# Sliding-window attention and an MLP in one kernel: taking the first batch's early casts off GpSimd, with new planning constants

## The chip, the cores and the metric

The kernel runs on one core of a Trainium2 chip. The metric is the device time of one execution in microseconds (us), as a median of several executions. The engines are called by their names in the profile: PE (TensorE matmul), PEld (its weight loads), DVE (VectorE), ACT (ScalarE), POOL (GpSimd) and SP (SyncE, which here only issues DMAs).

## The reference

Attention over 8 batches, 8 heads, 576 tokens and head dimension 64, with a causal window, and behind it a two-layer MLP on the joined heads:

```python
scores = scale * np.matmul(q, k.transpose(0, 1, 3, 2))
mask_plain = (rel >= 0) & (rel < 32)                          # heads 0..3
mask_dil = (rel >= 0) & (rel < 32 * 4) & (rel % 4 == 0)       # heads 4..7
scores = np.where(masks[None, :, :, :], scores, -1000000000.0)
attn = softmax(scores)                # written out with max, exp and sum
x = (attn @ v).transpose(0, 2, 1, 3).reshape(4608, 512)
h = x @ w_in                          # 512 -> 2048
out = np.maximum(0.01 * h, h) @ w_out # 2048 -> 512, float32
```

Inputs and output are float32; the kernel casts to float16 for the matmuls.

## The kernel before

**A planner writes the order of the work.** No loop order is given by hand. Each piece of work (a cast, a transpose, a group of matmuls, a DMA) is added as a task with an engine or several engines to choose from, a duration, a latency and the tasks it depends on. `forward` simulates the engines and appends tasks to each engine's list; `backward` works out how late each could begin; after `PASSES` rounds the shortest simulated schedule is kept, and its order is the program that each engine executes, first in, first out. A task with several engines goes to the one that is free, unless another would end it over 0.02 us earlier. From the time `CALM` on (38.8 us in the plan), durations are multiplied by `MARGIN` of the engine and latencies by `MARGIN['LAND']`. `WHEN` gives first priorities to the eight batches. So a changed duration or margin can move any task on any engine, with no line of its own in the diff.

**The loads come in a fixed order** on SP, with two of them on ACT's queue: `FIRST = 'r0 q01 v01 . q00 w0 v00 . w1 ...'`. Here `r0` is the last 64 tokens (512 to 575) of all heads of batch 0, tile `rest`; `q01` is q and k of group 1 of batch 0, the dilated heads; `q00` those of group 0, the plain heads; `v..` the same for v; `w0` to `w15` are the sixteen pieces of `w_in` and `w_out`, of which `w15` is the last.

**From a load to the scores.** float32 data land in staging tiles `stg` (q, k), `vst` (v) or, for the weights, in tiles not yet used otherwise (`gt`, `xt`, `wst`). A cast (L373 on DVE and POOL, L371 on ACT) writes float16 into `nat`, `rest`, `slots` or `w_in`/`w_out`. For batches 0 and 1, PE transposes `nat` (L640, into the banks `tp` and `fps`) and `rest` (L683), and copies (L386 on DVE, L384 on ACT) bring the result into `slots`, from which the scores are computed (L757 adds the mask, L761 multiplies). Exp on ACT (L768), sums and values on PE (L779), a reciprocal by Ln and Exp on ACT (L804, L806) and a product on DVE (L817, into `xt`) end a unit. There are two units for each pair of heads, and the pairs are taken in the order 2, 3 (dilated), 0, 1 (plain).

**The MLP.** `U` tasks (L836, L865) multiply `xt` by `w_in`, ACT applies the leaky ReLU into `gt` (L851, L877), and `D` tasks multiply `gt` by `w_out`: the first four token tiles plainly (L902, in four parts each, the last of which needs `w14` and `w15`), the others with a seven-product scheme (L992, sums L978 on DVE). The last three chunks do the first matmul by seven products as well (L1261); for that, four sums of the weights are formed on DVE (L1187).

**Which casts the change touches.** In `load_qk`, batch 0's casts (`first`) may go to POOL, DVE or ACT: 8 casts of 128x512, of which four belong to group 1. In `load_rest`, the four casts of 64x256 take the default of `cast`, POOL or DVE, for both early batches. The casts of v and of the weights are separate calls.

Of the kernel before, what the change touches and what calls it, by code (L numbers as in the profile page):

```python
# [16 lines left out]
WIN = 32  # L17
ROOM, LATE = 256, 0.5
RAMP = 0.0
WHEN = (0.0, 0.0, 40.0, 70.0, 100.0, 125.0, 150.0, 180.0)  # L20
PASSES = 9
MARGIN = {'ACT': 1.02, 'DVE': 1.062, 'POOL': 1.0, 'PE': 1.0, 'SP': 1.0, 'DMA': 1.133, 'LAND': 1.15}
CALM = 38.8
SEEDS = ()


def _margin(name, at):
    return MARGIN[name] if at > CALM else 1.0
FIRST = ('r0 q01 v01 . q00 w0 v00 . w1 w2 w3 w4 w5 w6 w7 w8 w9 w10 q11 w11 r1 v11 . w12 '
# [40 lines left out]
class _Plan:  # L70
# [5 lines left out]
    def add(self, eng, dur, lat, deps, fn, prio, soft=0.0, kind=""):  # L76
        choices = eng if isinstance(eng, tuple) else ((eng, dur),)
        t = _Task(choices, lat, deps, fn, prio, soft, len(self.tasks), kind)
        self.tasks.append(t)
        return t  # L80
# [169 lines left out]
def kernel(  # L250
# [14 lines left out]
    B, H, S, D = q.shape  # L265
# [20 lines left out]
    def at(tl, p0, p1, off, *dims):  # L286

        row = tl.ap[0][0]
        return bass.AP(tensor=tl.tensor, offset=tl.offset + p0 * row + off,
                       ap=[[row, p1 - p0]] + [list(d) for d in dims])  # L290

    def dram(t, off, *dims):
        return bass.AP(tensor=t.tensor, offset=t.offset + off, ap=[list(d) for d in dims])
# [61 lines left out]
    def load(queue, dst, src, n, size, deps, prio, late=None, slow=1.0):  # L355
        eng = ENG[queue]
        t = plan.dma(queue, 0.65, took(n, size) * slow, deps,
                     lambda e: eng.dma_start(dst, src), prio,
                     ((0.5 if prio < -1400 else LATE) if late is None else late)
                     + (RAMP * max(0.0, prio + 1500) / 40 if prio < -1400 else 0.0))  # L360
        t.fixed = prio < -1400
        t.rows = n / 16 + 2
        return t

    def cast(dst, src, n, deps, prio, engines=("POOL", "DVE"), slow=1.0):
        cost = {"POOL": 0.15 + n * 0.00102 * slow, "DVE": 0.07 + n * (0.00055 if slow == 1.0 else 0.0011),
                "ACT": (0.06 + n * 0.00087) * slow}

        def fn(e):
            if e == "ACT":  # L370
                nc.scalar.copy(out=dst, in_=src)  # L371
            else:
                ENG[e].tensor_copy(out=dst, in_=src)  # L373
        return add(tuple((e, cost[e]) for e in engines), None, 0.2, deps, fn, prio, 0.0, "cast")
# [18 lines left out]
    def ring(name, n, users):  # L393

        r = rings.setdefault(name, [])
        waits = r[-n] if len(r) >= n else []
        r.append(users)
        return (len(r) - 1) % n, waits
# [30 lines left out]
    def load_qk(b, g, prio):  # L429

        early, first = b < EARLY, b == 0
        base = (b * H + 4 * g) * HS
        stage, loads = [], []
        for o, src in ((0, q), (1, k)):
            if early:
                sn, s_old = ring("STG", NST, s_users := [])
            else:
                if "STG4" not in rings:
                    assert len(rings["STG"]) == 2 * NST
                    rings["STG4"] = rings["STG"][-NST:-1]  # L440
                sn, s_old = ring("STG4", NST - 1, s_users := [])
            st = stg[sn]
            if first and g == 1:
                lo = [load("ACT" if o else "SP", at(st, 0, 128, j * 256, [512, 2], [1, 256]),
                           dram(src, base + j * HS, [4 * D, 128], [2 * HS, 2], [1, 256]),
                           256, 1024, s_old, prio + 0.3 * j + 0.1 * o) for j in range(2)]
            elif early:
                lo = [load("SP", at(st, 0, 128, 0, [256, 4], [1, 256]),
                           dram(src, base, [4 * D, 128], [HS, 4], [1, 256]),
                           512, 1024, s_old, prio + 0.1 * o)] * 2  # L450
            else:
                lo = [load("SP", at(st, 32 * a, 32 * a + 32, 0, [32, 36], [1, 32]),
                           dram(src, base + (a // 2) * 2 * HS + (a % 2) * 32,
                                [D, 32], [32 * D, 36], [1, 32]),
                           1152, 128, s_old, prio) for a in range(4)]
            stage.append((st, s_users))
            loads.append(lo)
        for j in range(2):
            nn, n_old = ring("NAT", NNAT, n_users := [])
            na, c_qk = nat[nn], []  # L460
            for o in range(2):
                st, s_users = stage[o]
                if early:
                    dst = at(na, 0, 128, o * 512, [D, 2], [128, 4], [1, D])
                    src = at(st, 0, 128, j * 256, [512, 2], [D, 4], [1, D])
                    c = cast(dst, src, 512, [loads[o][j]] + n_old, prio,
                             ("POOL", "DVE", "ACT") if first else ("POOL", "DVE"))
                else:
                    c = cast(na[:, o * S:o * S + S], st[:, j * S:j * S + S], S,
                             loads[o] + n_old, prio, ("POOL",))  # L470
                c_qk.append(c)
                s_users.append(c)
            raw[b, 2 * g + j] = na, c_qk, n_users

    def load_rest(b, prio, queue="SP"):
        _, r_old = ring("REST", 1, r_users := [])
        sn, s_old = ring("STG", NST, s_users := [])
        st, c = stg[sn], []
        for o, src in ((0, q), (1, k)):
            lo = load(queue, at(st, 0, 64, o * 512, [64, 8], [1, 64]),  # L480
                      dram(src, b * H * HS + 512 * D, [D, 64], [HS, 8], [1, D]),
                      512, 256, s_old, prio + 0.1 * o)
            c += [cast(at(rest, 0, 64, o * 512 + 256 * g, [128, 2], [64, 2], [1, D]),
                       at(st, 0, 64, o * 512 + 256 * g, [64, 2], [128, 2], [1, D]), 256, [lo] + r_old, prio)
                  for g in (1, 0)]
        s_users += c
        raw[b, "rest"] = c, r_users
# [636 lines left out]
    for i, step in enumerate(steps):  # L1124
        kind, prio = step[0], clock[0] + 1 + i
# [11 lines left out]
    def attend(b, first, step):  # L1137
        if b >= EARLY:
            take_slots(b)
            for n, g in enumerate((1, 0)):  # L1140
                load_qk(b, g, first + 2 * step * n - 12)
                load_v(b, g, first + 2 * step * n - 11)
        for n, vi in enumerate(VISITS):
            if b < EARLY and n == b:
                turn_rest(b, first + step * n)
            turn(b, vi, first + step * n)
        if b == 0:
            banks = {2: three + [fps[0]], 3: three + [fps[0]], 0: three + hps[1:], 1: three + hps[1:]}
        else:
            banks = dict.fromkeys(VISITS, three + hps if b == 1 else three)  # L1150
        for n, vi in enumerate(VISITS):
            for u in range(2):
                unit(b, vi, u, first + step * n + 0.5 * step * u, banks[vi])
# [4 lines left out]
    def ups(c, x, n, batches):  # L1158
        if n == 192:
            pool = hps  # L1160
            for j in range(0, NJ, 2):
                up_pair(c, j, x, n, batches, all_acts[c], pool[j // 2 % len(pool)])
            return
        for j in range(NJ):
            wide_j = c == 0 and j in wide_banks
            ht = wide_banks[j] if wide_j else hps[h_at[0] % 2]
            h_at[0] += not wide_j
            up(c, j, x, n, batches, all_acts[c], ht, c == 0)
# [182 lines left out]
    for m in range(B // 2):  # L1351
        for c in range(3 * m, 3 * m + 3):
            gt_free[c] = []
        e, o = 2 * m, 2 * m + 1
        attend(e, WHEN[e], (WHEN[e + 1] - WHEN[e]) / 4 if e else 1.0)
        if 3 * m not in U_SEVEN:
# [3 lines left out]
        if m == 0:  # L1360
# [3 lines left out]
            ups(1, 0, 192, [e])  # L1364
            attend(o, WHEN[o], 5.0)
            ups(1, 192, 192, [o])
        else:
            attend(o, WHEN[o], 6.5)
            if 3 * m + 1 not in U_SEVEN:
# [23 lines left out]
    for t, u in zip(pe, pe[1:]):  # L1393
# [3 lines left out]
        while t.start > 0.5 and x + 0.3 < u.start:  # L1397
            n, step = (512, 0.3) if x + 0.4 < u.start else (256, 0.2)
# [41 lines left out]
```

## Time and profile before

| | us |
|---|---|
| median of 3 executions | 299.82 (299.55 to 300.49) |
| the profiled execution, its own time | 299.23 |
| span of its first to last instruction | 297.3 |
| busy in the span: PE / DVE / ACT / POOL | 285.0 / 221.7 / 218.9 / 142.7 |
| mean granted TensorE clock | 0.994 |

A timeline row gives the start, the time taken, the engine, the line, the operation, what it writes and reads, the shape and the count; several instructions of a kind in a row are merged. Brackets hold the idle time of the engine before it and what ended that. A `q` behind an engine's name is its sequencer, so `SPq DMA_DIRECT2D` is the issue of a transfer.

### The profile page before, as it was taken

To read this page: it belongs to the slowest core of one execution; us is meant where nothing else is said; L and a number is where in the kernel's file an instruction comes from. 1 tells how busy PE (TensorE), PEld (TensorE's weight loads), DVE (VectorE), ACT (ScalarE), POOL (GpSimd) and SP (SyncE) were. 2 spreads that over 40 slices of the span, in tenths; PEclk is the share of its full clock that TensorE was granted. 3 is DMA by queue.
4 is the path that set the end of the run, shared out by engine and by line. 5 is a ranking of instruction groups with operands and counts; after the bars stand their busy time and mean duration, and the time that the engine had idled before them with its cause. 6 is when DMAs were issued, how large, how long until landed. Compare 5 with 4: busy or idle time off the path is not lost.

```text
span 297.3 us, 7789 instructions
## 1 busy us (share of the span) xinstructions
PE 285.0 (96%) x2975; PEld 226.4 (76%) x2975; DVE 221.7 (75%) x406; ACT 218.9 (74%) x502; POOL 142.7 (48%) x201
## 2 busy tenths in 40 slices
PE   5779999999999999999999999998999999999995
PEld 2655677578667788777777787776789999999984
DVE  6785385986799899839768879899657786587742
ACT  1797578678988875878878866886877787877611
POOL 5455454197787848937866749996000100000000
PEclk9799999999999999999999999999999999999999
DMA  7999999889889988979899999440101210111033
GB/s 216 330 320 403 344 362 217 147 163 190 169 167 200 208 183 178 207 155 197 178 199 172 203 192 161 137 126 2 36 19 54 75 36 2 37 71 39 35 108 106
DMA packets 155973, 47.16 MB, mean 159 GB/s; under 512 B 136736, under 2 KB 153248, under 8 KB 155936
## 3 DMA queue, kind: packets, MB, share of 16 engines
q1 hardware_dynamic: 155248, 46.04, 65.1%
q10 hardware_dynamic: 688, 0.63, 0.7%
q8 instruction: 23, 0.38, 0.5%
q14 instruction: 14, 0.11, 0.1%
HBM read 37.22 MB, written 9.44 MB: 157 GB/s over the span
## 4 chain that ended last, share of the span: by engine, by line
PE 79%; DMA 8%; DVE 6%; ACT 3%; issue 2%; POOL 1%; SPq 0%; DVEq 0%; POOLq 0%
PE hps L836 22%; PE fps L992 22%; PE tp L992 8%; PE hps L1261 5%; PE ops L1261 3%; DMA xt<-in_moe_w_out_dram 3%; PE ops L779 3%; DMA vst<-in_v_dram 3%; PE fps L902 3%; PE ops L761 2%; PE hps L865 2%; DMA stg<-in_k_dram 2%; PE sps L779 2%; ACT gt L851 1%; DVE slots L386 1%
## 5 line engine op out<-in xcount | busy, mean ns | idle before, releaser
L836 PE MATMUL hps<-xt,w_in 128*128 128x384 f16 x488 | 95.1, 326 | 0.8 <-ACT gt L851 0.8
L992 PEld LDWEIGHTS <-gt 128*128 128x128 f16 x768 | 72.5, 98 | 9.5
L851 ACT ACTIVATE gt<-hps 128x384 f16<-128x384 f32 x122 | 59.1, 491 | 20.0 <-PE hps L836 18.8
L836 PEld LDWEIGHTS <-w_in 128*128 128x128 f16 x512 | 45.9, 98 | 23.2 <-issue 1.2
L373 POOL CAST slots<-vst 64x576 f16<-64x576 f32 (+2 forms) x60 | 54.4, 920 | 7.6 <-DVE slots L386 2.9
L992 PE MATMUL fps<-w_out,gt 128*128 128x256 f16 x368 | 47.0, 273 | 0.0
L373 POOL CAST nat<-stg 128x576 f16<-128x576 f32 (+1 forms) x55 | 40.6, 761 | 12.1 <-DVE xt L817 6.1
L772 DVE TENSOR_TENSOR ee<-ee,con 128x384 f16<-128x384 f16 (+1 forms) x48 | 23.7, 495 | 15.0 <-ACT ee L768 14.8
L806 ACT ACTIVATE rc<-rc 128x288 f32<-128x288 f32 x64 | 27.9, 442 | 0.9
L817 DVE TENSOR_TENSOR xt<-ops,rc 128x288 f16<-128x288 f32 x40 | 18.0, 450 | 12.7 <-ACT rc L806 8.3
L386 POOL COPY slots<-turned 64x64 f16<-64x64 f16 (+2 forms) x36 | 18.6, 525 | 15.1 <-DVE turned L605 7.5
L761 PEld LDWEIGHTS <-slots 128*128 128x128 f16 x320 | 18.7, 99 | 6.5 <-issue 1.4
L788 POOL TENSOR_TENSOR ee<-ee 128x128 f16<-128x128 f16 x9 | 5.3, 586 | 33.9 <-DVE ee L772 29.0
L779 PEld LDWEIGHTS <-slots 128*128 128x128 f16 x320 | 17.8, 97 | 4.7 <-POOL w_in L373 1.0
L768 ACT ACTIVATE ee<-ops 128x384 f16<-128x384 f32 (+1 forms) x39 | 19.5, 504 | 2.2 <-PE ops L761 1.8
L1021 ACT COPY stg<-fps 128x512 f32<-128x512 f32 (+1 forms) x24 | 12.8, 531 | 11.1 <-PE fps L992 10.4
L804 ACT ACTIVATE rc<-ops 128x288 f32<-128x288 f32 x39 | 15.8, 408 | 6.0 <-PE ops L796 3.1
L384 ACT COPY slots<-turned 64x512 f16<-64x512 f16 (+1 forms) x28 | 18.6, 663 | 1.9 <-DVE turned L605 1.5
L1288 ACT ACTIVATE gt<-slots 128x384 f16<-128x384 f32 x36 | 18.3, 526 | 0.9 <-DVE slots L1281 0.7
L605 DVE STREAM_TRANSPOSE turned<-nat 128x576 f16<-128x576 f16 x24 | 17.9, 760 | 0.0
L978 DVE TENSOR_TENSOR gt<-gt 128x1024 f16<-128x1024 f16 x21 | 17.2, 821 | 0.2 <-PE fps L992 0.2
L1261 PEld LDWEIGHTS <-stg 128*128 128x128 f16 x192 | 16.3, 98 | 0.3
(137 smaller groups left out, 556.6 us busy)
## 6 DMA issues: line engine op xcount, KB each, us to landing
out_dram<-osb SPq DMA_DIRECT2D x32, 256.0 KB, 2.5
stg<-in_q_dram SPq DMA_DIRECT2D x48, 144.0 KB, 3.4
stg<-in_k_dram SPq DMA_DIRECT2D x48, 144.0 KB, 3.2
vst<-in_v_dram SPq DMA_DIRECT2D x14, 288.0 KB, 4.3
gt<-in_moe_w_in_dram SPq DMA_DIRECT2D x6, 512.0 KB, 6.7
vst<-in_v_dram SPq DMA_DIRECT2D x24, 128.0 KB, 2.9
stg<-in_q_dram SPq DMA_DIRECT2D x3, 512.0 KB, 9.0
stg<-in_k_dram SPq DMA_DIRECT2D x3, 512.0 KB, 9.4
```

Source lines behind the costliest of these rows:

```text
L373: ENG[e].tensor_copy(out=dst, in_=src)
L384: nc.scalar.copy(out=dst, in_=src)
L386: ENG[e].tensor_copy(out=dst, in_=src)
L761: nc.tensor.matmul(p_bank[:, c:c + w], slot(tn, KB + 128 * s, 0, 128, [1, 128]), slot(tn, qx, 0, 128, *qd), start=first or not by_pe, stop ...
L768: lambda e: nc.scalar.activation(out=et[:, 0:n], in_=p_bank[:, 0:n], func=AF.Exp, scale=SCALE), prio)
L772: lambda e: nc.vector.tensor_tensor(out=et[:, 0:n], in0=et[:, 0:n], in1=con[:, table:table + n], op=ALU.mult), prio,
L779: nc.tensor.matmul(at(dst, 0, 128, o, *od), lhs(s), et[:, c:c + w], start=i == 0, stop=i == len(steps) - 1, skip_group_check=True)
L806: lambda e: nc.scalar.activation(out=rt, in_=rt, func=AF.Exp, scale=-1.0), prio)
L836: nc.tensor.matmul(ht[:, 0:n], at(w_in, 0, 128, vi * DFF + j // 2 * 256 + j % 2, [2, 128]), at(xt[m % 2], 0, 128, vi * 1152 + x0 + x, [1, n]),
L851: lambda e: nc.scalar.activation(out=gt[c % NG][:, j * n_c + x:j * n_c + x + n], in_=ht[:, 0:n], func=AF.Prelu, alpha=0.01),
L992: nc.tensor.matmul(bk[:, x:x + HN], tl[:, off + j * step:off + j * step + 128], rhs(j), start=first and x == 0 and j == 0, stop=j == HJ - ...
L1261: nc.tensor.matmul(b[:, i * HT:i * HT + HT], lhs(v, j0 + i), rhs(v), start=first and i == 0 and v == 0, stop=i == 1 and v == 1, skip_group ...
```

## The change

Batch 0's casts of the dilated heads' q and k, and of the last tokens, no longer have POOL among their engines: they may go to DVE or ACT. Batch 1's casts keep theirs. In the planner, a DVE cast of q, k, last tokens or weights counts 0.07 + n * 0.00076 us in place of 0.07 + n * 0.00055, so 0.46 in place of 0.35 us at n = 512. Beside it, constants of the planner differ: from `CALM` on, durations on DVE count 1.099 times (1.062 before), on POOL 1.001 times, latencies 1.129 times (1.15 before); `CALM` itself is 35.4 us (38.8 before), and the first priority of batch 5 is 126.4 (125.0 before).

```diff
-WHEN = (0.0, 0.0, 40.0, 70.0, 100.0, 125.0, 150.0, 180.0)
+WHEN = (0.0, 0.0, 40.0, 70.0, 100.0, 126.4, 150.0, 180.0)
 PASSES = 9
-MARGIN = {'ACT': 1.02, 'DVE': 1.062, 'POOL': 1.0, 'PE': 1.0, 'SP': 1.0, 'DMA': 1.133, 'LAND': 1.15}
-CALM = 38.8
+MARGIN = {'ACT': 1.02, 'DVE': 1.099, 'POOL': 1.001, 'PE': 1.0, 'SP': 1.0, 'DMA': 1.133, 'LAND': 1.129}
+CALM = 35.4
...
     def cast(dst, src, n, deps, prio, engines=("POOL", "DVE"), slow=1.0):
-        cost = {"POOL": 0.15 + n * 0.00102 * slow, "DVE": 0.07 + n * (0.00055 if slow == 1.0 else 0.0011),
+        cost = {"POOL": 0.15 + n * 0.00102 * slow, "DVE": 0.07 + n * (0.00076 if slow == 1.0 else 0.0011),
                 "ACT": (0.06 + n * 0.00087) * slow}
...
                     c = cast(dst, src, 512, [loads[o][j]] + n_old, prio,
-                             ("POOL", "DVE", "ACT") if first else ("POOL", "DVE"))
+                             (("DVE", "ACT") if g else ("POOL", "DVE", "ACT")) if first else ("POOL", "DVE"))
...
             c += [cast(at(rest, 0, 64, o * 512 + 256 * g, [128, 2], [64, 2], [1, D]),
-                       at(st, 0, 64, o * 512 + 256 * g, [64, 2], [128, 2], [1, D]), 256, [lo] + r_old, prio)
+                       at(st, 0, 64, o * 512 + 256 * g, [64, 2], [128, 2], [1, D]), 256, [lo] + r_old, prio,
+                       ("POOL", "DVE") if b else ("DVE", "ACT"))
                   for g in (1, 0)]
```

## The prediction

> **What bounds the kernel now.** I read the page first, then the busy time by stretches, then who PE waits for, then the timeline of the first 15 us, and last the chain of waits with the timelines around the places where it leaves PE.
>
> ```profile
> PE 285.0 (96%) x2975; PEld 226.4 (76%) x2975; DVE 221.7 (75%) x406; ACT 218.9 (74%) x502; POOL 142.7 (48%) x201
> 0.00:10.00 10.00, 5.47 (x26) 2.10 (x27) 6.96 (x14) 2.35 (x5) 5.92 (x15) 1.00 0.81 249
> 10.00:20.00 10.00, 8.87 (x127) 7.40 (x127) 7.86 (x18) 9.03 (x23) 5.40 (x10) 0.83 1.00 307
> 20.00:30.00 10.00, 8.31 (x88) 5.56 (x87) 6.05 (x14) 8.28 (x21) 4.79 (x7) 1.00 1.02 398
> 30.00:50.00 20.00, 19.98 (x222) 14.80 (x222) 11.65 (x28) 14.53 (x36) 9.97 (x15) 1.00 1.10 324
> 70.00:90.00 20.00, 19.27 (x195) 13.57 (x194) 16.34 (x30) 18.06 (x45) 15.28 (x22) 1.00 0.94 178
> 200.00:210.00 10.00, 9.04 (x82) 6.38 (x80) 10.00 (x19) 6.71 (x16) 5.94 (x7) 1.00 0.08 28
> 210.00:230.00 20.00, 20.00 (x238) 17.25 (x237) 13.14 (x31) 15.25 (x38) 0.43 (x1) 1.00 0.06 20
> ```
>
> The columns behind the length are busy us of PE, PEld, DVE, ACT and POOL, then the granted clock, the DMA engines' busy share and GB/s. PE is the bound from 30 us on: it lacks 0.02 us of 20 between 30 and 50, 0.73 between 70 and 90, 0.96 between 200 and 210. Before 30 us it lacks 4.53 + 1.13 + 1.69 = 7.35 us. The matmuls are fixed work, so the end moves only by PE's lost time: nearly all that can be had lies in the first 30 us, where the change works, and what it may spoil lies behind them.
>
> The start shows who holds PE up:
>
> ```profile
> 5.27 0.49 DVE L373 CAST rest<-stg 64x256 f16<-64x256 f32 x2 [0.77 <-DMA stg<-in_q_dram]
> 6.45 0.28 DVE L373 CAST rest<-stg 64x256 f16<-64x256 f32 x1 [0.70 <-DMA stg<-in_k_dram]
> 6.48 0.84 POOL L373 CAST rest<-stg 64x256 f16<-64x256 f32 x1 [2.45 <-DMA stg<-in_k_dram]
> 6.66 2.06 DVE L373 CAST nat<-stg 128x512 f16<-128x512 f32 x2
> 7.28 1.16 POOL L373 CAST nat<-stg 128x512 f16<-128x512 f32 x2
> 7.46 0.29 PE L683 MATMUL hps<-con,rest 64*128 64x64 f16 x4
> 7.78 0.27 ACT L384 COPY slots<-hps 128x128 f16<-128x128 f16 x1 [5.76 <-PE hps L683]
> 8.78 0.40 PE L640 MATMUL tp<-con,nat 128*128 128x128 f16 x4 [1.03 <-DVE nat L373]
> 9.46 0.58 ACT L384 COPY slots<-fps 64x512 f16<-64x512 f16 x1 [0.19 <-DVE slots L386]
> 10.31 0.47 PE L757 MATMUL sps<-con 128*128 128x192 f16 x3
> L373 DVE CAST nat<-stg x2: 411/1068/1726, 6.7 to 7.0; 128x512 f16<-128x512 f32 x2
> L373 POOL CAST nat<-stg x2: 605/605/605, 7.3 to 7.8; 128x512 f16<-128x512 f32 x2
> ```
>
> The last two rows group the casts of that stretch by line (least, median and most ns, first and last start). The two DVE casts are alike, yet one took 0.411 us and the other, from 7.0 to 8.72, 1.726 us: just while POOL cast `rest` (to 7.32) and two halves of `nat` (to 8.44). PE's transposes wait for it at 8.78, DVE's copies queue behind it, and the first scores come at 10.31.
>
> **The change part by part.**
>
> *First casts.* Eight go: four of 64x256, four of 128x512, of which POOL had one and two. On DVE a small one takes 0.28 (row 6.45), a large one 0.411 unopposed. On ACT a large one has this row:
>
> ```profile
> L371 ACT CAST nat<-stg x1: 610/610/610, 15.5 to 15.5; 128x512 f16<-128x512 f32 x1
> ```
>
> For ACT's 64x256 in this layout there is no row; I bound it by 0.27 (its 128x128 copy at 7.78) and 0.58 (its 64x512 copy at 9.46) and take 0.35, near the smaller, since the elements per row are 256 against 128 and 512. If both engines take one of k's last tokens at 6.45, these end near 6.8 in place of 7.32, and the transposes at 7.46 can begin at about 6.9. DVE then casts from 6.75: the four large ones end at about 7.15, 7.55, 7.95 and 8.35 if ACT takes none. The data are there: the casts of before had begun by 7.0 and, for POOL's second, by 7.28 + 0.605 = 7.9. The half of q for which PE waits at 8.78 is third of the four at worst, done at 7.95 rather than 8.72, and second at best, done at 7.55. So PE's transposes of it come 0.8 to 1.2 us earlier. ACT's added casts are covered by its idle time of 5.76 us before 7.78; a large one taken at 7.2 would hold ACT's first copies until 7.8, where they begin now, so it costs nothing even then. If DVE still has its fourth cast to do when the copies are ready, they wait another 0.41. First scores: 1.0 us earlier, between 0.4 and 1.2.
>
> Here a rule of the Trainium skill can be weighed. The row says that a DVE cast lost 1.726 - 0.411 = 1.3 us to three POOL casts in turn. SBUF — State Buffer, section "SBUF: two separate sides", says that VectorE in a two-port mode and GpSimd hold a shared port pair exclusively for a whole instruction, whoever starts first. By that rule alone the DVE cast would be held only by the cast in progress, to 7.32, and would have ended at about 7.75, so the change would bring 0.2 us; by the row it brings about 1.0, and the row decides.
>
> *From there to 30 us.* The chain of dependent work (copies, exp, reciprocals, DVE's products) starts earlier as a whole. It stays ahead of the weights:
>
> ```profile
> 27.16 0.87 POOL L373 CAST w_in<-wst 128x512 f16<-128x512 f32 x1 [0.61 <-DMA wst<-in_moe_w_in_dram]
> 29.99 2.85 PE L836 MATMUL hps<-xt,w_in 128*128 128x384 f16 x16 [0.82 <-ACT gt L851]
> ```
>
> The last cast of `w_in` is done at 28.03; PE's use of it, from 29.99, waits for ACT's evictions instead, so 1.0 us earlier it still finds its weights, with 0.96 to spare. The casts of v on POOL stay, and no large DVE cast of the first group stands beside them now. Full gain at 30 us: 1.0.
>
> *30 to 51 us, where some is given back.*
>
> ```profile
> 41.02 9.40 DMA xt<-in_moe_w_out_dram
> 50.47 0.88 POOL w_out L373
> 51.39 0.38 PE fps L902
> 50.51 1.26 PE L902 MATMUL fps<-w_out,gt 128*128 128x512 f16 x4
> 52.00 1.02 PE L902 MATMUL fps<-w_out,gt 128*128 128x512 f16 x4
> 52.86 0.34 PE L757 MATMUL ops<-con 128*128 128x64 f16 x3
> 53.22 0.34 PE L757 MATMUL hps<-con 128*128 128x384 f16 x2
> ```
>
> The first three rows are of the chain of waits (start, us, what), the others of PE's timeline. The loads keep the DMA engines full (share 1.10), so the last weight piece lands at 50.42 whatever the casts do. PE issues three matmuls of a group from 50.51 and the fourth, which needs that piece, at 51.39; the group takes 1.26 us where the next takes 1.02: a stall of 0.24. A PE that comes early can use that, and whatever of batch 1's scores (the work at 52.86 and 53.22) moves ahead of it: from 52.86 to 53.22 is 0.36 for each, and batch 1 has three such units open, 1.1 us at most, as far as ACT and DVE, which are also earlier, have copied its q and k. So 0.24 to 1.0 of the gain passes. I take 0.75, nearer the upper end, since PE lacks 0.02 of 20 us here now and so has a queue of work rather than gaps: given back 0.25.
>
> *The costs and margins.* These move the order behind 35 us. What they can win or lose there has these rows:
>
> ```profile
> PE ops L761 <- DVE xt L817: 0.7, 1, 0.7
> PE ops L779 <- ACT rc L804: 0.6, 1, 0.6
> PE sps L761 <- DVE xt L817: 0.2, 1, 0.2
> 194.38 1.61 DVE stg L1187
> 197.87 1.66 DVE stg L1187
> ```
>
> These are PE's waits behind 60 us (total, times, longest), then two pieces of the chain. DVE is 10.00 of 10 us busy between 200 and 210, and PE waits there for its products twice, 0.7 + 0.2 = 0.9. Counting DVE 3.5% longer sets PE's users of DVE results later in the list, with other matmuls before them, which is the right direction for those 0.9; but the new order is another order, and one more weight sum of 1.66 us ahead of a product that PE needs would cost as much. Bounds -0.9 and +1.66; I take -0.25, since PE has other work in the list to put there (from 210 to 230 us it is busy without a gap). `WHEN` and POOL's 1.001 I cost at nothing: they change a priority that later rounds replace, and POOL's durations by 0.1%.
>
> *Sum:* -1.0 + 0.25 - 0.25 = -1.0. The profiled execution's own time is 299.23, of which 297.3 is span and 1.9 lies around it, unchanged; it would come to 298.2. It lies 0.59 below the median of the runs shown, 299.82; by that median, the forecast is 298.8.
>
> **The rivals.**
>
> *The DMA hides it.* All but the 0.24 us stall is lost in front of the last weight piece at 51.39, and the margins do nothing. For it: the share of 1.10 and the chain, which passes through that transfer. Against it: PE has no gap before that point, so the work between is not exhausted. Time 299.82 - 0.24 = 299.6, or up to 299.0 if half passes. Chance 0.26.
>
> *DVE becomes the late bound.* The planner, with longer DVE times, puts one of the four weight sums (1.66 us) ahead of a product for which PE waits between 194 and 207 us. It decides once PE's wait for `xt` there exceeds 0.9 + 1.0 us, the gain. With little of the front gain kept that is 299.82 + 1.66 - 0.24 = 301.2; with two sums and the front's 0.75, 302.4; with one and 0.75, 300.7. For it: DVE is already full there, 10.00 of 10. Against it: only 0.9 of PE's time is lost to that now, and the sums have 10 us of room before. Chance 0.21.
>
> *The late waits vanish as well.* If the 0.9 us behind DVE and the 0.6 behind ACT go, this adds 1.25 to the forecast: 297.6. Chance 0.12.
>
> *The clock rises earlier.* Between 10 and 20 us the granted clock is 0.83 in the mean, and like groups of matmuls are slower at first:
>
> ```profile
> 10.62 0.48 PE L761 MATMUL sps<-slots 128*128 128x96 f16 x5
> 14.41 0.33 PE L761 MATMUL ops<-slots 128*128 128x96 f16 x5
> ```
>
> A mean of 0.83 over 10 us is half rate for 3.4 of them, so a full rate would save PE at most 1.7 us; its work there alternates with ACT's exps, which would not be faster, so I let 0.7 pass: 298.1. Against it: the idle 1.03 us before 8.78 only shrinks. The Trainium skill (TensorE: Matmul & The Clock Gate, "What's actually happening") says that activity in a free-running window of about 3.4 us sets the rate, so that its place may differ from run to run; the 3.4 us above agree with its length. Chance 0.05.
>
> **How the numbers follow.** The forecast (298.2 to 298.9) has 0.36. A measurement of this kernel tells about 0.3%, 0.9 us, from no change. Faster by more: forecast, late waits and clock, 0.36 + 0.12 + 0.05 = 0.53. Within: the DMA case, 0.26. Slower: 0.21. The range from 297.4 to 301.3 takes in the late waits (297.6) and the DVE case with one sum (301.2), and leaves out two sums and both extra gains together.
>
> **What would show it.** In the profile after: no POOL cast before v's at about 9.4; no DVE cast over 0.5 us before 9; the first L640 on `tp` by 8.0 and the first scores (L757) near 9.3 rather than 10.31; PE's U work on the second half of `w_in` from about 29.0; the last weight piece landing still near 50.4, with PE's wait before it under 0.5. Wrong would be: first scores after 10.0 (ACT or DVE took too long), a wait of over 0.7 us before 51.4 (the DMA hides it), or PE waits for `xt` of over 1.9 us between 194 and 210.

## The result: slower by 3.7 us, and the profile after

| | before | changed |
|---|---|---|
| median of 6 executions each | 299.69 (299.02 to 301.25) | 303.43 (302.69 to 304.08) |
| changed / before | | 1.0118, 95% interval 1.0089 to 1.0147 |
| the profiled execution, its own time | 299.23 | 304.08 |
| its span | 297.3 | 302.3 |
| busy PE / DVE / ACT / POOL | 285.0 / 221.7 / 218.9 / 142.7 | 284.5 / 227.7 / 217.6 / 141.9 |

The forecast was 298.8, with a range from 297.4 to 301.3. The sign is wrong, and the time lies outside the range.

The busy time by stretches of the changed kernel, in the columns explained with the forecast (length, then PE, PEld, DVE, ACT, POOL, granted clock, DMA share, GB/s):

```profile
0.00:10.00 10.00, 5.79 (x39) 2.71 (x40) 5.60 (x14) 3.57 (x7) 4.02 (x13) 1.00 0.80 244
10.00:20.00 10.00, 6.94 (x109) 5.24 (x107) 7.77 (x18) 8.95 (x23) 4.63 (x8) 1.00 1.08 342
20.00:30.00 10.00, 9.04 (x93) 5.97 (x93) 6.30 (x15) 8.52 (x22) 5.83 (x8) 1.00 1.03 403
30.00:50.00 20.00, 19.46 (x217) 14.53 (x217) 10.25 (x24) 14.49 (x35) 12.18 (x20) 1.00 1.10 315
50.00:70.00 20.00, 18.90 (x215) 13.70 (x213) 16.11 (x25) 13.63 (x32) 10.22 (x16) 1.00 0.80 137
70.00:90.00 20.00, 18.95 (x197) 13.79 (x195) 15.13 (x29) 16.33 (x42) 14.55 (x20) 1.00 0.92 173
130.00:150.00 20.00, 19.24 (x179) 14.05 (x178) 15.65 (x22) 14.97 (x35) 14.10 (x21) 1.00 0.93 197
150.00:170.00 20.00, 19.07 (x198) 14.20 (x198) 15.05 (x29) 16.47 (x37) 11.18 (x17) 1.00 0.94 173
170.00:190.00 20.00, 18.58 (x189) 14.47 (x188) 18.20 (x28) 13.07 (x32) 13.09 (x18) 1.00 0.80 145
200.00:210.00 10.00, 9.92 (x96) 7.23 (x95) 10.00 (x14) 9.45 (x21) 8.19 (x9) 1.00 0.37 94
```

And three stretches of the kernel before, which the forecast did not show:

```profile
130.00:150.00 20.00, 20.00 (x197) 14.88 (x196) 15.95 (x28) 16.00 (x38) 14.55 (x22) 1.00 0.90 178
150.00:170.00 20.00, 20.00 (x209) 15.16 (x206) 15.06 (x29) 16.70 (x40) 13.59 (x20) 1.00 0.97 195
170.00:190.00 20.00, 20.00 (x205) 15.85 (x203) 17.17 (x30) 14.59 (x34) 14.55 (x17) 1.00 0.91 179
```

Read the PE column as lost time. Behind 30 us the kernel before loses 1.78 us of PE in all its stretches. The changed one loses 6.45: 0.54 + 1.10 + 1.05 up to 90 us, 0.76 + 0.93 + 1.42 between 130 and 190 where before lost nothing, 0.08 between 200 and 210, and 0.24 and 0.33 in two stretches not shown (110 to 130, 210 to 230). That is 4.67 of the 5.0 us by which the two spans differ. (The medians differ by 3.7: the profile of before is of a quick execution, that of the changed kernel of the longest of its six.) The other 0.3 is there at 30 us already: the second half of `w_in` is used from 30.30, where it was 29.99. So the place to look is behind 30 us. There the change moves no named cast. It has only numbers of the planner, and so another order.

The timeline of the changed kernel has the new waits of PE; each row's bracket is PE's idle time before it and what ended that (lines stand one higher than before: L817 is now L818, L978 is L979):

```profile
51.95 0.34 PE L758 MATMUL ops<-con 128*128 128x64 f16 x3 [1.10 <-DVE xt L818]
88.23 1.05 PE L993 MATMUL tp<-w_out,gt 128*128 128x256 f16 x8 [0.59 <-DVE gt L979]
150.93 0.35 PE L762 MATMUL sps<-slots 128*128 128x64 f16 x5 [1.68 <-DVE xt L818]
184.51 1.05 PE L993 MATMUL fps<-wst,gt 128*128 128x256 f16 x8 [1.29 <-DVE gt L979]
...
146.03 3.17 DVE L386 COPY slots<-turned 64x64 f16<-64x64 f16 x1
149.22 0.69 DVE L979 TENSOR_TENSOR gt<-gt 128x1024 f16<-128x1024 f16 x1
149.82 0.68 DVE L1030 TENSOR_TENSOR osb<-fps,stg 128x512 f32<-128x512 f32 x1
150.42 0.45 DVE L818 TENSOR_TENSOR xt<-sps,rc 128x288 f16<-128x288 f32 x1
...
146.02 0.69 POOL L612 COPY slots<-turned 128x576 f16<-128x576 f16 x1
146.67 2.50 POOL L373 CAST nat<-stg 128x576 f16<-128x576 f32 x4
...
181.57 2.89 DVE L979 TENSOR_TENSOR gt<-rest,gt 128x1024 f16<-128x1024 f16 x1
181.27 0.83 POOL L373 CAST slots<-vst 64x576 f16<-64x576 f32 x1
182.03 2.96 POOL L373 CAST nat<-stg 128x576 f16<-128x576 f32 x4
```

The two longest, 1.68 and 1.29 us, have one cause in sight. At 146.03 a DVE copy of 64x64, which takes 0.16 us at its shortest, takes 3.17; it ends just after a run of five POOL operations, at 149.17. At 181.57 a sum of a kind that takes 0.68 at 180.36 takes 2.89: it was ready in the midst of a POOL cast of v and waited through it and through three of the four casts behind. In the first case the product `xt` for which PE waits stands three places behind the copy in DVE's queue. It is the signature that the forecast saw at 7.0 us before, now at a place where PE has nothing else to do. The view counts the held time as busy DVE, and DVE shows 6.0 us more busy than before with two instructions fewer.

### The profile page after: what moved, and what is told of

The parts are those of the page before. It is cut to its first block, busy times and chain, and to the rows that moved or that the text cites. A ratio compares the mean times of both kernels' runs of the same rounds, so it can differ in the third digit from the quotient of the medians.

```text
span 302.3 us, 7787 instructions
## 1 busy us (share of the span) xinstructions
PE 284.5 (94%) x2974; PEld 225.3 (75%) x2974; DVE 227.7 (75%) x404; ACT 217.6 (72%) x499; POOL 141.9 (47%) x206
## 4 chain that ended last, share of the span: by engine, by line
PE 63%; DVE 10%; SPq 6%; issue 6%; ACT 5%; DMA 5%; POOL 4%; POOLq 0%; ACTq 0%
PE fps L993 16%; PE hps L837 14%; SPq L358 6%; PE tp L993 6%; PE hps L1262 5%; PE fps L903 4%; PE hps L866 4%; PE ops L1262 3%; DMA stg<-in_k_dram 3%; DVE gt L979 2%; POOL nat L373 2%; PE ops L780 2%; ACT gt L852 2%; DVE slots L386 1%; POOL slots L373 1%
## 5 line engine op out<-in xcount | busy, mean ns | idle before, releaser
L373 POOL CAST slots<-vst 64x576 f16<-64x576 f32 (+2 forms) x62 | 52.4, 856 | 12.6 <-DVE nat L373 5.4
L373 POOL CAST nat<-stg 128x576 f16<-128x576 f32 (+1 forms) x53 | 38.9, 758 | 16.8 <-DVE t L933 7.9
L773 DVE TENSOR_TENSOR ee<-ee,con 128x384 f16<-128x384 f16 (+1 forms) x48 | 25.2, 525 | 8.8 <-ACT ee L769 8.3
L818 DVE TENSOR_TENSOR xt<-ops,rc 128x288 f16<-128x288 f32 x40 | 17.7, 444 | 15.5 <-ACT rc L807 14.3
L789 POOL TENSOR_TENSOR ee<-ee 128x128 f16<-128x128 f16 x13 | 8.2, 629 | 35.5 <-DVE ee L773 35.4
L1022 ACT COPY stg<-fps 128x512 f32<-128x512 f32 (+1 forms) x22 | 11.6, 528 | 13.6 <-PE fps L993 10.6
L993 PE MATMUL fps<-wst,gt 128*128 128x256 f16 x128 | 16.4, 272 | 1.3 <-DVE gt L979 1.3
L979 DVE TENSOR_TENSOR gt<-gt 128x1024 f16<-128x1024 f16 x21 | 16.7, 797 | 0.9 <-PE fps L993 0.9
```

The costliest lines, as they stand in the source:

```text
L773: lambda e: nc.vector.tensor_tensor(out=et[:, 0:n], in0=et[:, 0:n], in1=con[:, table:table + n], op=ALU.mult), prio,
L979: lambda e: ENG[e].tensor_tensor(out=dst, in0=a, in1=b, op=op),
L993: nc.tensor.matmul(bk[:, x:x + HN], tl[:, off + j * step:off + j * step + 128], rhs(j), start=first and x == 0 and j == 0, stop=j == HJ - ...
```

## The experiments

### Which part of the change costs

Four kernels split the change, and three more take single numbers. Each time stands against that of the kernel before on the same chip; the chips differ between some of the kernels. The first takes only the engine choices from the diff:

```diff
-                             ("POOL", "DVE", "ACT") if first else ("POOL", "DVE"))
+                             (("DVE", "ACT") if g else ("POOL", "DVE", "ACT")) if first else ("POOL", "DVE"))
...
+                       ("POOL", "DVE") if b else ("DVE", "ACT"))
```

> The kernel before with only the choice of engines changed (first batch's casts of last tokens and of the dilated q, k on VectorE or ScalarE); costs and margins as before. In the planner's list PE's order from 22 us on is then the same as before, word for word. Theory A (the loss is the new order of the work behind 30 us, which the cost and the margins make): 299.7 within 0.6, PE's lost time behind 30 us at most 2 us as before. Theory B (the casts themselves cost: ScalarE's casts stand ahead of exps, and the lateness goes through to the end): 301 or more.

Measured: 299.60 against 299.55 (12 and 29 executions), ratio 0.9998, interval 0.9969 to 1.0028. The casts make no difference beyond 0.3% either way. In its profile, of an execution of 300.68, PE loses 3.07 us behind 30 us, more than the 2 us that were expected.

The second keeps the order of before word for word and only hands POOL's three early casts to other engines, so that no replanning is mixed in (the lines that mark the casts are left out here):

```diff
...
     order = plan.run()
+    to = iter(("ACT", "DVE", "ACT"))
+    for t in sorted(tagged, key=lambda t: t.start):
+        if t.eng == "POOL":
+            t.eng = next(to)
```

> The order of the kernel before, all engines' lists word for word, except that the three casts that GpSimd had among the first eight go to ScalarE, VectorE and ScalarE at their old places in time. Port theory (the 1.73 us cast is held by GpSimd): no VectorE cast above 0.5 us before 9 us, first scores at 9.4 in place of 10.3. If the first batch's gain passes to the end, 298.8; if the loads (last weight piece at 50.4) hide it, 299.2 to 299.7; 301 or more if casts on ScalarE cost.

Measured: 300.13, ratio 1.0014 (0.9997 to 1.0031). The hold was gone, since both DVE casts from 6.61 took 0.89 together, but the first scores came no earlier, at 10.44 and not at the 9.4 expected. PE's transposes at 10.22 had waited 1.45 us for ACT's copy at 9.59. That copy had waited for DVE, whose copies from 9.14 stood behind the cast moved to it (0.43 us from 8.68), and that cast stood behind a copy for which DVE had been idle for 0.92 us. So the early gain was lost to the place of the moved DVE cast, and ACT's moved cast, at 10.20, came later.

The third and fourth take the numbers: all of them with POOL's casts kept, and all but the longer cast (the last pair of lines).

```diff
-WHEN = (0.0, 0.0, 40.0, 70.0, 100.0, 125.0, 150.0, 180.0)
+WHEN = (0.0, 0.0, 40.0, 70.0, 100.0, 126.4, 150.0, 180.0)
...
-MARGIN = {'ACT': 1.02, 'DVE': 1.062, 'POOL': 1.0, 'PE': 1.0, 'SP': 1.0, 'DMA': 1.133, 'LAND': 1.15}
-CALM = 38.8
+MARGIN = {'ACT': 1.02, 'DVE': 1.099, 'POOL': 1.001, 'PE': 1.0, 'SP': 1.0, 'DMA': 1.133, 'LAND': 1.129}
+CALM = 35.4
...
-        cost = {"POOL": 0.15 + n * 0.00102 * slow, "DVE": 0.07 + n * (0.00055 if slow == 1.0 else 0.0011),
+        cost = {"POOL": 0.15 + n * 0.00102 * slow, "DVE": 0.07 + n * (0.00076 if slow == 1.0 else 0.0011),
```

> The kernel before with only the planner's numbers changed (VectorE's cast cost, margins, first priority); GpSimd keeps its casts. Theory A (the new order costs): 303 to 304, with PE's waits at about 52, 88, 151 and 184 us as in the changed kernel, about 5 us of lost time behind 30 us. Theory B (the casts cost): about 300.

Measured: 303.53, ratio 1.0124 (1.0094 to 1.0153): the whole loss. PE's longest waits in this kernel behind its warm-up at the start, as a list of who waited for whom (total, times, longest):

```profile
PE sps L761 <- DVE xt L817: 1.7, 1, 1.7
PE fps L992 <- DVE gt L978: 1.3, 1, 1.3
PE ops L757 <- DVE xt L817: 1.1, 1, 1.1
```

They are the same three as in the changed kernel, and PE loses 5.74 us behind 30 us. The long DVE instructions are the same, too: the copy at 144.31 takes 3.17 us again, the sum at 179.82 takes 2.88.

> The kernel before with the margins, the calm time and the first priority of the changed kernel, but VectorE's cast cost and the engines as before. If the margins make the bad order: 302 to 304. If the longer VectorE cast does it: 299.5 to 300.5. If any change of the plan costs because the margins before fitted one order only: 301 to 303, with waits at other places than in the changed kernel.

Measured: 301.96, ratio 1.0074 (1.0038 to 1.0109). This order has no DVE instruction held for 3 us; its loss comes in waits of up to 1.0 us, the longest of them before PE's work at 38.85, 1.02 us for ACT's eviction.

Then single numbers: the longer cast, POOL's 1.001, and DVE's 1.099, each with all else as before.

> The kernel before with only VectorE's cast cost changed (0.00076 an element in place of 0.00055). If the bad order needs cost and margins together: 299 to 300.5. If any change of a number spoils the order that the old margins fitted: 301 to 303, by long holds of VectorE beside runs of GpSimd casts at some place or other.

Measured: 303.18 (4 executions), ratio 1.0106 (1.0055 to 1.0158). It has other waits at other places, nine of 0.16 to 0.74 us between 66 and 211 us. They are not behind DVE instructions held for 2 us or more, as had been expected.

> The kernel before with one constant of the margins changed by a thousandth (GpSimd's, 1.0 to 1.001); the planner's order is the same up to 175 us and another behind it. If the order is fragile, that alone moves the time by up to 1 to 2 us; if the numbers act by their size, 299.6 within 0.5.

Measured: 298.79, ratio 0.9972 (0.9939 to 1.0005): no cost, and no gain that can be told from none.

> The kernel before with only VectorE's margin changed (1.062 to 1.099). If longer VectorE times make the bad order: 301.5 to 303.5. If the margin's size does nothing by itself: 299 to 300.5.

Measured: 306.23 (4 executions), ratio 1.0213 (1.0156 to 1.0271): as bad as the whole change at least, which took 1.018 times the kernel before on the same chip (below). That is worse than expected. Its longest waits:

```profile
PE sps L761 <- DVE xt L817: 1.5, 1, 1.5
PE hps L865 <- ACT gt L877: 1.3, 1, 1.3
PE sps L779 <- DVE ee L772: 1.1, 1, 1.1
```

So the parts don't add up: the cast's longer count gives +1.06%, the margins +0.74%, both together +1.24%, and one of those margins alone +2.1%. The intervals of the first three are too wide to tell their sum from 1.24%, but the single margin lies clear of the margins together. What a number costs is not in its size but in which of many orders falls out, and each of these orders has its waits at places of its own.

### Where the early gain of the casts goes

In the kernel with the casts alone the gain is there at first and gone later. An eviction is ACT's move of a finished block from the bank `hps` into `gt`. The first and the 25th of them in the kernel before:

```profile
26.11 0.49 ACT L851 ACTIVATE gt<-hps 128x384 f16<-128x384 f32 x1 [1.23 <-PE hps L836]
...
62.31 1.12 ACT L877 ACTIVATE gt<-hps 128x384 f16<-128x384 f32 x2
```

And in the kernel with the casts alone, with PE's rows in between where it stops for weights:

```profile
24.32 0.49 ACT L852 ACTIVATE gt<-hps 128x384 f16<-128x384 f32 x1 [1.23 <-PE hps L837]
28.79 0.50 PE L837 MATMUL hps<-xt,w_in 128*128 128x384 f16 x2 [1.62 <-DVE w_in L373]
52.09 0.85 PE L903 MATMUL fps<-w_out,gt 128*128 128x512 f16 x2 [0.68 <-DVE w_out L373]
63.96 1.10 ACT L878 ACTIVATE gt<-hps 128x384 f16<-128x384 f32 x2
```

The first eviction is 1.8 us early. PE then waits 1.62 us for a piece of `w_in` and 0.68 for one of `w_out`, and the 25th eviction is 1.65 us late. From there to the end of the span it takes 297.3 - 62.31 = 235.0 us before, 298.9 - 63.96 = 234.9 here and 235.1 in the kernel with the three casts moved. So with this order the time is decided up to there, and by when the weights are in. The last cast of `w_out` on POOL began at 50.47 before and at 51.64 here, and two profiles of the unaltered changed kernel have it 3.0 us apart, at 49.36 and 52.34. A single profile therefore can't tell a load that is late by chance from an effect of the casts. But five kernels with all their weights have PE work in the same order from 22 us to this point (before, the casts alone, the three casts moved, POOL's 1.001, and the last kernel below). In these the cast began anywhere between 49.4 and 54.0 (right behind the landing of its load, at 50.42 before and at 53.97 in the last kernel below), the 25th eviction came 11.8 to 12.3 us behind it in each, and the rest took 234.6 to 235.1.

To test that the loads eat the gain, two kernels load only the first half of each weight piece and cast both halves from it: half the weight bytes are gone, and the output is another. The second also has the engine choices.

```diff
-            src = dram(moe_w_out, 128 * x, [2 * DM, 128], [1, 1024])
+            src = dram(moe_w_out, 128 * x, [2 * DM, 128], [1, 512])
...
-        t = load("SP", st, src, 128, 4096, old, prio, 1.0, 1.0)
+        t = load("SP", st[:, 0:512], src, 128, 4096, old, prio, 1.0, 1.0)
...
-            c = cast(dst[:, x + 512 * i:x + 512 * i + 512], st[:, 512 * i:512 * i + 512], 512, [t],
+            c = cast(dst[:, x + 512 * i:x + 512 * i + 512], st[:, 0:512], 512, [t],
```

> The kernel before, every engine's list word for word, but each weight piece's load brings only its first 512 of 1024 columns, and both halves of the piece are cast from them: 4 MB less to load, and other weights, so another output. The baseline for the next one. If the loads bind up to 62 us: 2 us or more below the kernel before.

> The same with casts_alone's choice of engines. If the loads hid the casts' gain (first evictions 1.8 us earlier in casts_alone, all lost again by 62 us): 0.8 to 1.8 us below half_weights. If something else takes it (DVE, ACT or PE's order): within 0.4 us of half_weights.

Measured on one chip: 298.41 with half the weight bytes (ratio 0.9979, 0.996 to 0.9999) and 297.73 with the casts as well (0.9935, 0.9909 to 0.9961). Neither of the two stops for `w_out` any more: the last piece is there when POOL casts its half of it, at 41.12 and 42.39, and DVE casts the other half at its place in the order, at 49.12 and 48.47. The first eviction comes at 25.55 and 24.50, 1.05 us apart; 0.79 of that is left at the 25th (61.20 and 60.41) and 0.7 at the end of the spans (296.2 and 295.5).

Both expectations were missed, if the second barely. Without half the bytes the kernel gains 1.0 us and not 2, so the loads hold this order up less than was thought. And the casts bring 0.7 us by the medians, just under the 0.8 to 1.8 expected if the loads hid the gain. The two intervals against before overlap, but the two kernels' own times, twelve each, differ by 0.8 us in the mean, with a 95% interval of 0.4 to 1.2. So the casts' early gain is real once the loads are out of its way. With all the weights the interval of the casts alone, 0.9969 to 1.0028, does not exclude a gain of 0.9 us; that the loads take it rests on PE's waits and on the landings above as much as on the times.

### The two long waits

The order of the changed kernel stays word for word, and the eight POOL casts that stand beside the two held DVE instructions (four of batch 5, four of batch 7) go to ACT:

```diff
...
     order = plan.run()
+    for b, g in ((5, 1), (7, 0)):
+        for t in tagged[b][4 * g:4 * g + 4]:
+            t.eng = "ACT"
```

> The changed kernel's order word for word, but the eight casts of 128x576 that GpSimd does in a row from 146.7 and from 182.0 us (batch 5's plain heads, batch 7's dilated heads) go to ScalarE at their planned places. Theory A1 (PE's long waits at 150.9 and 184.5, 1.7 and 1.3 us, come from one VectorE instruction being held for a whole run of GpSimd casts, 3.2 and 2.9 us): both waits go, no VectorE instruction above 1.5 us there, 1.5 to 3 us less than the changed kernel: 300.5 to 302. Theory A2 (the new order is too tight in any case, VectorE would be late there also without the runs): the waits stay, 303 to 304.

Measured: 302.73, ratio 1.0101 (1.0068 to 1.0135), above the 300.5 to 302 expected and hardly less than the changed kernel's 1.0118, though PE's two long waits were gone. Since the two had not run side by side, both ran once more on one chip:

> The changed kernel, unaltered, on the same chip as the next one. 1.012 of the kernel before, within 0.002.

> The same kernel as runs_to_scalar, beside the changed kernel. By their profiles, ScalarE's evictions ran 0.8 and 1.5 us earlier behind the two places, and 0.4 later at one place behind: if that is what the time is made of, 1.5 to 2.2 us less than the changed kernel on the same chip (ratio to before about 1.006). If the holds are not what the time is made of: within 0.5 us of it.

Measured: 305.00 for the changed kernel (1.018, 1.0134 to 1.0226) and 302.71 with the runs on ACT (1.0104, 1.0059 to 1.0149). The changed kernel missed the 1.012 expected of it on this chip, and so did the other its 1.006, but the difference of 2.3 us is a little more than the 1.5 to 2.2 expected. The longest waits of PE behind 40 us with the runs on ACT, and the two DVE instructions that had been held (lines stand four higher than before):

```profile
52.41 0.34 PE L761 MATMUL ops<-con 128*128 128x64 f16 x3 [0.69 <-DVE xt L821]
152.18 0.35 PE L783 MATMUL ops<-ee,slots 128*128 128x64 f16 x5 [0.55 <-ACT rc L808]
205.42 0.22 PE L800 MATMUL ops<-ee,con 128*128 128x128 f16 x1 [0.53 <-POOL ee L792]
...
145.73 0.72 DVE L386 COPY slots<-turned 64x64 f16<-64x64 f16 x1
180.32 1.03 DVE L982 TENSOR_TENSOR gt<-rest,gt 128x1024 f16<-128x1024 f16 x1
```

The copy takes 0.72 in place of 3.17 and the sum 1.03 in place of 2.89, both long waits are gone, and PE loses 4.40 us behind 30 us in place of the 6.80 of the changed kernel's profile on that chip. That is 2.3 us of the 6.1 by which the changed kernel was slower there. The other 3.8 are not these two holds. PE's many small waits behind 30 us account for 2.6 of them (4.40 against 1.78 before), 2.0 of that up to 90 us; no run took them apart one by one.

Nor does a hold cost by itself. The kernel before has one too:

```profile
105.95 1.79 DVE L386 COPY slots<-turned 64x64 f16<-64x64 f16 x1
```

It stands beside POOL's copies and casts, and PE loses nothing between 90 and 110 us, since it has other work then. What the new order changed is that two such holds fell in front of results that PE needed next.

### DVE beside POOL's runs, by itself

A small kernel gives DVE one operation while POOL has 0, 1, 2 or 4 casts of 128x576 in its queue, for five kinds of DVE operation. Each such pairing is called a cell.

> Measures the hold by itself: no attention and no MLP, the output is zeros. Twenty cells, each opened by ScalarE: GpSimd does 0, 1, 2 or 4 casts of 128x576 float32 in a row, and VectorE, some 0.2 us behind, one operation: a 64x64 float16 copy, a product of two SBUF operands (128x384), a 128x512 cast from float32, a product of PSUM and SBUF (128x288), a copy from PSUM (128x512). If VectorE is held for the whole run: the first three grow by about 0.6 us for each cast (4 casts: 2 us and more), the last two not at all. If it gets its turn behind the cast in progress: at most 0.6 us more, whatever the run's length.

Its timeline, with the DVE copy alone and beside one, two and four casts, and the run of four:

```profile
3.86 0.16 DVE L34 COPY ddst<-dhal 64x64 f16<-64x64 f16 x1
4.61 0.58 DVE L34 COPY ddst<-dhal 64x64 f16<-64x64 f16 x1 [0.58 <-ACT dhal L49]
5.67 0.58 DVE L34 COPY ddst<-dhal 64x64 f16<-64x64 f16 x1 [0.48 <-ACT dhal L49]
7.46 0.58 DVE L34 COPY ddst<-dhal 64x64 f16<-64x64 f16 x1 [1.21 <-ACT dhal L49]
...
7.34 2.86 POOL L53 CAST pdst<-psrc 128x576 f16<-128x576 f32 x4 [0.39 <-ACT psrc L48]
```

The copy is held to the end of the cast in progress, 0.58 us, whether one or four are queued. A product of 128x384 goes from 0.36 to between 0.75 and 0.80, and a cast of 128x512 from 0.43 to between 0.65 and 0.68; the two kinds that read PSUM keep their 0.46 and 0.69. That speaks against a plain "held by the whole run". But these casts all wrote one tile and so left 0.06 us between them. The second version gives each cast its own tile, so that POOL runs without a pause:

> As held_by_runs (the output is zeros, no attention, no MLP), but GpSimd's casts write to different tiles, so that none waits for the one before it and they follow each other without a gap, as in the kernel; runs of 1, 2, 4 and 8, with VectorE's operation 0.1 or some 0.5 us behind the first. If the gap of 0.06 us between dependent casts let VectorE in: now it is held for several casts, up to the whole run (4 casts: over 2 us). If it is let in behind the cast in progress anyway: at most 0.8 us in all cells, and the long holds in the kernel have another cause.

Measured: again at most the cast in progress (copy 0.58, product 0.76, cast 0.68 to 0.88). The third takes sequences like those of the changed kernel, strided copies (which read every fourth column) ahead of casts, with DVE's operation meant to become ready at three moments:

> As held_by_runs (output zeros, no attention, no MLP), with the kernel's sequences on GpSimd: five operations in a row on different tiles, of casts 128x576 (c), strided copies 128x576 (t) and 64x512 (u), strided casts 64x576 (v), as ccccc, tcccc, uutcc, vcccc, ttttt; VectorE's 64x64 copy or 128x384 product follows the first by about 0.1, 0.3 or 0.5 us. If the kind of the operation in progress (a strided copy or cast) lets GpSimd keep the port: 2 us and more in tcccc, uutcc, vcccc and at most 0.8 in ccccc. If it is the moment at which VectorE asks: long holds at one of the three delays in all sequences. If neither: at most 0.8 everywhere, and the cause stays open.

In the trace the moments are others than meant: ACT opens a cell as soon as POOL has left the first tile of the one before, so from the second cell on DVE's operation mostly becomes ready during the second or third POOL operation of the run before. Of the 30 cells 28 took at most 0.83 us, and two did not; the first row is one of the 28:

```profile
28.31 0.24 DVE L50 COPY ddst<-dhal 64x64 f16<-64x64 f16 x1 [2.23 <-ACT dhal L62]
31.41 7.96 DVE L50 COPY ddst<-dhal 64x64 f16<-64x64 f16 x1 [2.87 <-ACT dhal L62]
...
80.02 3.30 DVE L52 TENSOR_TENSOR dhal<-dhal,ddst 128x384 f16<-128x384 f16 x1 [2.81 <-ACT dhal L62]
```

So a hold over many operations exists outside the kernel as well, and it is rare. The copy of 7.96 us waited through 13 POOL operations of three cells and was let in when POOL ran out of work, as the copy of 3.17 us in the kernel was. The product of 3.30 us got in after five operations, the sum of 2.89 us in the kernel after three. Of the 28 others, one met no POOL operation, one (a copy of 0.76 us at 22.24) was held through the next operation too, and 26 were held for no longer than the one in progress.

In the two long cells DVE was ready 0.024 and 0.028 us before POOL began its next operation. Of the four cells where it was ready 0.055 to 0.063 us ahead, three got in behind the current operation and the one at 22.24 did not. In the changed kernel, though, the sum at 181.57 became ready in the midst of a cast and was held all the same. What decides between one operation and many stays open.

### A better version?

The casts with POOL's 1.001, the only two parts that cost nothing alone:

> The casts of the change on the order that pool_number_alone made (GpSimd's margin 1.001, all other numbers as before). As pool_number_alone, 0.997 of the kernel before, if the loads hide the casts' gain; 0.993 to 0.996 if some passes; 1.00 if pool_number_alone was chance.

Measured: 299.62, ratio 1.0024 (0.9999 to 1.0049). That fits the last of the three expectations, that the 0.997 of POOL's 1.001 was chance. No version found here beats the kernel before.

## Why the prediction was wrong, step by step

**First casts: right at the start, wrong on ACT.** No POOL cast comes before v's at 9.45, no DVE cast before 9 us takes over 0.41, PE's L641 on `tp` begins at 8.00 and the first scores at 8.67 rather than 10.31. But in the changed kernel this is gone a few microseconds later:

```profile
8.67 0.33 PE L758 MATMUL sps<-con 128*128 128x192 f16 x3
9.53 0.62 ACT L371 CAST nat<-stg 128x512 f16<-128x512 f32 x1
9.56 0.35 PE L762 MATMUL sps<-slots 128*128 128x96 f16 x5 [0.56 <-ACT slots L384]
10.89 0.50 ACT L769 ACTIVATE ee<-sps 128x384 f16<-128x384 f32 x1
11.79 0.47 ACT L371 CAST slots<-vst 64x256 f16<-64x256 f32 x1
13.58 0.18 PE L780 MATMUL ops<-ee,slots 128*128 128x32 f16 x1 [0.82 <-DVE slots L373]
```

The step that said that ACT's casts cost nothing looked at ACT's idle time before 7.78 only. The planner placed a cast of `nat` on ACT at 9.53, ahead of the copy at 10.18 and the exps; in the kernel with the casts alone ACT has no such cast there, and its first exp starts at 10.11, not 10.89 (0.26 of these 0.78 us is there at the first scores already, at 8.41). What this one place costs was not measured by itself. Of the terms, ACT's 64x256 took 0.41 where I took 0.35.

**To 30 us and on to 51 us: wrong, the loads take it.** "Full gain at 30 us" rested on 0.96 us to spare at `w_in`. In the changed kernel the gain was gone before that: the group that began at 29.99 begins at 30.30, and waits for ACT (0.82). In the kernel with the casts alone the chain was 1.8 us early, and there PE waited 1.62 us at `w_in` itself and 0.68 at `w_out`. So the rival "the DMA hides it" had the casts right, which measured no change. Its sign, a wait of over 0.7 us before the last weight piece, was all but met there (0.68), though not in the changed kernel, whose weights came early. The rival placed the loss only at `w_out`, and in that profile most of it came at `w_in`. Those waits, the steady distance from the landing of the last weights to the 25th eviction, and the gain of 0.8 us with half the weights point to the loads.

**Costs and margins: the term that failed.** I took -0.25, with bounds of -0.9 and +1.66; measured alone it is +1.24%, 3.7 us. I bounded it by the waits that the trace of before had and by one weight sum put in a bad place. Both bounds assume that the new order is the old one with one thing moved. It is a different order everywhere behind 35 us, and the old one lost only 1.78 us of PE there, so another order had little to win and much to lose; of the five kernels that keep before's casts and change numbers, four are slower and the fifth, POOL's 1.001, can't be told from before. The late waits that I meant to win back did vanish: between 200 and 210 us PE loses 0.08 in place of 0.96. Other waits behind 30 us took their place, and 4.67 us more in the balance of the two profiles.

**The slower rival** had the right engine and the wrong mechanism. PE waited for nothing between 190 and 200 us and for 0.08 between 200 and 210, so no weight sum stood in its way there. DVE was held beside runs of POOL casts at 146 and 182 us, which the row at 7.0 us of before had shown in kind, and which I used for the gain at the start and not as a risk behind it. Its price would have been readable: a hold of a few casts at 0.6 us each, in front of a product that PE needs.

**The clock** did rise earlier in this execution (1.00 between 10 and 20 us, 0.83 before), but PE stood idle for 3.06 us of that stretch, in front of copies, casts and exps. What an early rise is worth was not isolated. Over 90 executions of the kernel before on four chips, the 65 with a mean clock of 0.997 or more took 299.4 us on average and the 25 with less 300.2, which is near the 0.7 that this rival let pass and far less than the loss.

## What to carry to other kernels

Where the matmul engine loses under 2 us in 230, treat any change of a planner's constants as drawing a new order, and price it by how much such an order can lose, not by the waits that the present one has; a hand-fixed order with one thing moved is the cheap way to test an idea without that draw. An early gain ahead of a stretch in which the loads are full is worth nothing until one has followed it to every piece of weights on the way. And a DVE operation on SBUF that stands next to a run of GpSimd operations can be held for all of it, which costs where the next result is needed at once: look for instructions that take many times the least of their form, since the view counts them as busy.

## What the runs showed of the hardware

A DVE operation on SBUF beside a run of POOL operations is usually held for the one in progress at most (a 64x64 copy took 0.58 us in place of 0.16), and now and then for several or all of the run: 3.17 and 2.89 us in the changed order, for the same two instructions in three profiles, 7.96 and 3.30 us alone. Operations that read PSUM kept their 0.46 and 0.69 us. The Trainium skill (SBUF — State Buffer, "SBUF: two separate sides") has the shared port pair as an exclusive lock for the whole instruction of whoever starts first. The 0.58 us, and 26 of the 30 cells of the third version, agree with it; the 3.17 and 7.96 us do not follow from it, since several POOL instructions started and ended while DVE waited, and there the measurement decides.

The time at which the weights are in differs by execution: in two profiles each of the same two programs, the last cast of `w_out` on POOL began at 49.36 and 52.34, and at 52.42 and 50.31. The kernel before itself ran from 297.4 to 302.5 us in all but one of its executions, with a median of 298.9 to 299.8 in each comparison.
